# A fused decay attention and MLP kernel: another order for the opening, and SyncE's requests in written order

## The chip, the cores and the metric

The kernel runs on one core of a Trainium2 chip as one launch. The core has five engines with queues of their own: TensorE (PE: matmuls, with weight loads PEld), VectorE (DVE), ScalarE (ACT), GpSimd (POOL) and SyncE (SP), which here does nothing but issue DMA requests. The metric is the device time of a run in microseconds, the median of three runs for the kernel before.

## The reference

Attention over 8 batches of 8 heads, 576 positions and 64 dimensions, then a two-layer MLP over the 4608 tokens.

```python
scores = scale * np.matmul(q, k.transpose(0, 1, 3, 2))
log_f = np.log(np.clip(f, 0.0001, 1.0))
cum = np.cumsum(log_f, axis=-1)
decay = cum[:, :, :, None] - cum[:, :, None, :]
scores = np.where(causal, -1000000000.0, scores + decay)
scores = scores - np.max(scores, axis=-1, keepdims=True)
attn = np.exp(scores)
attn = attn / (np.sum(attn, axis=-1, keepdims=True) + 1e-09)
x = np.matmul(attn, v)          # then heads side by side: 4608 x 512
h = np.maximum(x @ w_in, 0.0)   # w_in 512 x 2048
out = h * h @ w_out             # w_out 2048 x 512
```

## The kernel before

**Data.** There are 64 heads. q and k of a head arrive transposed, side by side (64 x 2 x 576). Heads 0 to 13 ("whole", `NWHOLE = 14`) use two tiles each: `rounded` (name `rk`, q and k rounded to the float32r type by a casting DMA that POOL issues, `load_rounded`, L252) for the row maxima, and `whole` (name `rl`, full float32, requested by SP, `load_whole`, L259) for the scores. Below the 64 rows of q and k lie constant rows and decay rows: the running sum of log f, split in a high and a low row, so that one matmul gives scores with their decay. A further row of `whole` takes the row maxima, so that they too come off in the matmul. From head 14 on ("split" heads) q, k and v are cut into rounded parts by the engines (`prep`, `split_v`), and SP loads the raw tile (`load`, L237).

**Decay (`decay`, L134 to L148).** SP loads f for all 64 heads (L132). DVE clamps it (L138), ACT takes the logarithm (L139) and loads the table of the exponential (L142), DVE forms the running sum (L143), its rounded part (L146) and the rest (L147), in the tile `qkraw`. `load_cum` (L240) brings a head's two rows to `rounded` and `whole`: for head 0 straight from that tile, one request a row (L244), for the others from a copy in DRAM (`cum_dr`, stored by `store_cum`, L152; read at L246).

**Row maxima (`max_units`, L303 to L335).** Six units a head. Each is a matmul (L313) into one of two PSUM banks and a masked reduction on DVE (L319, two instructions in the profile) into a column `tcol`; when a block of queries is done SP writes it as a row into `whole`, or into `rounded` for split heads (L325, `rl<-tcol` or `rk<-tcol`). There are five such requests a head.

**Scores.** A head has six units (`NU = 6`), one a slot. `score` (L337) multiplies (L346, the mask at L348; L352 and L355 in split heads) and takes the exponential on ACT (L362); two slots later `av_part` multiplies with v (L411; L388 to L390 in split heads). `finish` divides by the row sums, by way of DRAM (requests L436, L441, L444), for two heads at a time.

**Weights (`weight_ops`, L164).** A generator that takes the 32 blocks of w_in and w_out through five steps each, on ACT (`wmag`, L181), DVE (L192, L197, L202, L204), then a rounded copy on ACT (L209) and the rest on POOL (L210). Each step ends in a `yield`; the requests (`stage`, L172, 512 KB each) stand in the fourth step and run `DEPTH` blocks ahead.

**MLP.** `mlp1` (L471; matmuls L477) and `mlp2` (L491; L500) run in half steps that `fill` places between the attention's work from slot 60 on; output goes out by SP (L507).

**What sets the order.** The code writes work slot by slot, from slot -12 on: `score`, `av_part`, `finish`, then the events of the slot's first half, weight steps (`cv`), MLP work, and the second half's. In slots -12 to -7 there is one weight step a slot, in -6 to -1 two, in 0 to 47 1.2, after that 2.5 (`RATES`, L549). `MAXIMA` (L555) places the units of row maxima of head h at half slots from `(h - 1) * NU`: those of head 0 in slots -6 to -4, of head 1 in slots 0 to 2. At the end `in_order` (L18) ties each instruction of PE, ACT, DVE and POOL to the one written before it on the same engine. SP is not in that list: a scheduler places its requests.

**The opening, L92 to L158 and L635 to L644.** POOL writes the masks `mz` and `eye`, the constant columns of `vhs`, and the constant rows of `whole[0]`, `rounded[1]` and `whole[1]` (`constant_rows`, L115: two memsets and, for `whole`, a select), and only then issues the casting loads of heads 0 and 1. DVE writes those of `rounded[0]`. SP requests f, the first weights, q and k of head 0 and, after the decay, the decay rows.

Of the kernel before, what the change touches and what calls it, by code (L numbers as in the profile page):

```python
# [9 lines left out]
F32 = mybir.dt.float32  # L10
F32R = mybir.dt.float32r
I32 = mybir.dt.int32
BF16 = mybir.dt.bfloat16
AF = mybir.ActivationFunctionType
ALU = mybir.AluOpType


def in_order(tc, engines):  # L18

    last = {}  # L20
    for i in tc.nc.cur_bb.bb.instructions:
# [12 lines left out]
def decay_attention_relu2_kernel(  # L34
# [18 lines left out]
    nc = tc.nc  # L53

    NH, D, _, S = qk.shape
    P = 2 * D
# [25 lines left out]
    def bank(use):  # L82
# [6 lines left out]

    MW = 448  # L90
    mz = cpool.tile([P, MW], BF16, name="mz")
    nc.gpsimd.memset(mz, 0.0)  # L92
    nc.gpsimd.affine_select(
        out=mz[:, MW - P:], in_=mz[:, MW - P:], pattern=[[-1, P]],
        compare_op=ALU.is_ge, fill=-1e9, base=0, channel_multiplier=1,
    )

    eye = wk.tile([P, 448], F32, name="p").bitcast(BF16)[:, :P]
    nc.gpsimd.memset(eye, 0.0)
    nc.gpsimd.affine_select(  # L100
        out=eye, in_=eye, pattern=[[-1, P]],
        compare_op=ALU.not_equal, fill=1.0, base=0, channel_multiplier=1,
    )

    rounded = [cpool.tile([P, 2, S], F32R, name=f"rk_{i}") for i in range(2)]
    whole = [wk.tile([P, 2, S], F32, name="rl") for _ in range(2)]

    vhs = [cpool.tile([P, NJ, D + 2], F32R, name=f"vh_{i}") for i in range(2)]  # L110

    def f32(x):
        return x if x.dtype == F32 else x.bitcast(F32)

    def constant_rows(engine, x, ones=True):  # L115

        engine.memset(f32(x[D:, 0]), -1.0 / SCALE)
        engine.memset(f32(x[D:, 1]), 0.0)
        if ones:
            k = f32(x[D:, 1])  # L120
            nc.gpsimd.affine_select(
                out=k, in_=k, pattern=[[0, S]], compare_op=ALU.not_equal, fill=1.0, base=-2,
                channel_multiplier=1,
            )


    cum_dr = dr.tile([NH, 2, S], F32, name="cum_dr", bufs=1)
    fr = wk.tile([P, NCC, S], F32, name="xt0", bufs=1)
    cum = []

    def load_f():
        nc.sync.dma_start(out=fr[:NH, 0, :], in_=f)  # L132

    def decay():  # L134
        ft, zt, ct = (fr[:NH, i, :] for i in range(3))
        nc.vector.memset(zt, 0.0)
        constant_rows(nc.vector, rounded[0], False)
        nc.vector.tensor_scalar(ft, ft, 1e-4, 1.0, ALU.max, ALU.min)  # L138
        nc.scalar.activation(out=ft, in_=ft, func=AF.Ln)  # L139
        warm_exp = wk.tile([P, 8], F32, name="tcol")  # L140
        nc.vector.memset(warm_exp[:, :1], 0.0)
        nc.scalar.activation(out=warm_exp[:, :1], in_=warm_exp[:, :1], func=AF.Exp)  # L142
        nc.vector.tensor_tensor_scan(ct, zt, ft, 0.0, ALU.add, ALU.add)  # L143
        chl = wk.tile([P, 2, S], F32R, name="qkraw", bufs=1)
        ch, cl = chl[:, 0, :], chl[:, 1, :]
        nc.vector.tensor_copy(out=ch[:NH], in_=ct)  # L146
        nc.vector.tensor_tensor(out=cl[:NH], in0=ct, in1=ch[:NH].bitcast(F32), op=ALU.subtract)  # L147
        cum.extend(x.bitcast(F32) for x in (ch, cl))  # L148

    def store_cum():  # L150
        for i, x in enumerate(cum):
            nc.sync.dma_start(out=cum_dr[:, i, :], in_=x[:NH])  # L152

    for x in vhs:
        nc.gpsimd.memset(x[:, :, D:D + 2].bitcast(F32), 1.0)
    constant_rows(nc.gpsimd, whole[0])
    constant_rows(nc.gpsimd, rounded[1], False)
    constant_rows(nc.gpsimd, whole[1])  # L158


    NW = 2 * NF
    split_w = []

    def weight_ops():  # L164

        staged, mags = {}, {}

        def stage():
            i = len(staged)
            if i < NW:  # L170
                raw = staged[i] = wk.tile([P, 2 * DM], I32, name=f"w{i}", bufs=1)
                nc.sync.dma_start(out=raw, in_=(w_in, w_out)[i % 2][i // 2].bitcast(I32))  # L172
# [12 lines left out]
        yield  # L185
        magnitude(0)
        yield
        for i in range(NW):
            low, high = words(i)
            mag = mags.pop(i)  # L190

            nc.vector.tensor_scalar(mag, mag, MAG_LOW, MAG_HIGH, ALU.max, ALU.min)  # L192
            yield
            w = wk.tile([P, DM], F32, name="osb")
            wi = w.bitcast(I32)

            nc.vector.tensor_scalar(  # L197
                wi, mag.bitcast(I32), 3, 0x3FFFFFFF, ALU.logical_shift_left, ALU.bitwise_and,
            )
# [4 lines left out]
            nc.vector.scalar_tensor_tensor(wi, low, 29, wi, ALU.logical_shift_right, ALU.bitwise_or)  # L204
            while len(staged) < min(i + 1 + DEPTH, NW):
                stage()
            yield
            hl = wk.tile([P, 2, DM], F32R, name=f"w{i}", bufs=1)
            nc.scalar.copy(out=hl[:, 0], in_=w)  # L209
            nc.gpsimd.tensor_tensor(out=hl[:, 1], in0=w, in1=hl[:, 0].bitcast(F32), op=ALU.subtract)  # L210
            split_w.append(hl)
            yield
# [6 lines left out]
    def convert(n):  # L219

        for _ in range(n):
            next(weights, None)
# [7 lines left out]
    NU = len(UNITS)  # L230
# [8 lines left out]

    def load_cum(h, k):  # L240

        if h == 0:
            for i, c in enumerate(cum):
                nc.sync.dma_start(out=f32(k[D + i:D + i + 1, :]), in_=c[h:h + 1])  # L244
        else:
            nc.sync.dma_start(out=f32(k[D:D + 2, :]), in_=cum_dr[h])  # L246

    def load_rounded(h):

        x = rounded[h % 2]  # L250
        state[h] = dict(r2=x[:, 0], kl0=x[:, 1], p={})
        nc.gpsimd.dma_start(out=x[:D], in_=qk[h])  # L252
# [293 lines left out]

    RATES = (1, 2, 1.2, 2.5)  # L549
    LAG = 2  # L550
    NA = H * NU

# [58 lines left out]
    def at(n, half, do, *args):  # L611
        events.setdefault((n, half), []).append(lambda: do(*args))
# [6 lines left out]
    for h in range(NH):  # L619
        split = h >= NWHOLE  # L620
        if split:
            at((h - 2) * NU + LOAD, 0, load, h)
            for part in range(4):
                at((h - 1) * NU + SPLIT[part], 1, prep, h, part)
        else:
            if h > 1:
                at((h - 3) * NU + 3, 0, load_rounded, h)
                at((h - 2) * NU + 5, 1, load_whole, h)
        at((h - 1) * NU + VLOAD, 1, load_v, h)
        at((h - 1) * NU + VSPLIT, 1, split_v, h)  # L630
        for i, x in enumerate(MAXIMA[split]):
            at((h - 1) * NU + int(x), int(2 * x) % 2, max_unit, h, i)
    for b in range(B):
        at(ready[b] - 2, 0, split_x, b * S // T, b + 1)
    load_f()  # L635
    load_rounded(0)
    convert(1)
    load_whole(0)
    decay()
    load_cum(0, rounded[0][:, 1])  # L640
    load_cum(0, whole[0][:, 1])
    store_cum()
    load_rounded(1)
    load_whole(1)  # L644
    for n in range(-2 * NU, last_slot + 1):
        live = 0 <= n < len(slots)
        split_last()
        if live:
            h, u = slots[n]
# [21 lines left out]
    while halves[0] < 2 * NCHUNK * NF:  # L671
        mlp_half(B)
    mlp2(*steps[-1])
    in_order(tc, [getattr(mybir.EngineType, e) for e in ("PE", "Activation", "DVE", "Pool")])


# [37 lines left out]
```

## Time and profile before

| | us |
|---|---|
| median of 3 runs (lowest to highest) | 1255.66 (1254.82 to 1255.89) |
| the profiled execution | 1255.36 |
| its span, first to last instruction | 1253.3 |
| PE busy | 1193.5 (95%) |
| DVE busy | 785.1 (63%) |
| ACT busy | 702.0 (56%) |
| POOL busy | 372.4 (30%) |

The mean granted TensorE clock of the execution is 0.995. In a profile line of the timeline the first number is the start in microseconds from the span's beginning, the second the length, then the engine (a q after its name marks its request queue), the line of the kernel, the operation, and `out<-in` by tile names without their numbers. In brackets stands how long the engine was idle before, and what ended that. A row of waits reads: who waited for what, total, times, longest.

### The profile page before, as it was taken

The numbers are of one execution on the slowest core, as the hardware profiler recorded it, in microseconds if no ns is written. First come the engines' busy times: TensorE is split into PE (matmuls) and PEld (weight loads), VectorE is DVE, ScalarE is ACT, GpSimd is POOL, SyncE is SP. The second block draws the span as 40 slices with busy tenths as digits, with TensorE's granted clock in tenths as the row PEclk, the third lists the DMA queues.
The fourth block names the chain that finished last, engine by engine and source line by source line (L and its number), as shares of the span: only waits on it lengthen the run. The fifth ranks groups of instructions, "written<-read, shape, count | busy, mean of one in ns | idle before, by whom it ended". The sixth has DMA issues, their size and how long they took to land.

```text
span 1253.3 us, 23182 instructions
## 1 busy us (share of the span) xinstructions
PE 1193.5 (95%) x7652; PEld 1051.8 (84%) x7652; DVE 785.1 (63%) x2042; ACT 702.0 (56%) x1720; POOL 372.4 (30%) x512
## 2 busy tenths in 40 slices
PE   3877899999999999999999999999999999999998
PEld 2544687888989899999899989998998989999997
DVE  7658776666666767666656566667665766532332
ACT  3545455556666666665565556666666666632332
POOL 4323223333333333333322233334333333200000
PEclk9999999999999999999999999999999999999999
DMA  8857631112121112121201121211121212000000
GB/s 199 193 129 176 177 87 26 51 32 57 41 55 33 48 37 57 40 57 26 55 18 52 31 57 32 55 34 52 40 57 41 57 41 52 17 27 1 18 18 17
DMA packets 115639, 71.90 MB, mean 57 GB/s; under 512 B 97384, under 2 KB 97384, under 8 KB 115520
## 3 DMA queue, kind: packets, MB, share of 16 engines
q1 hardware_dynamic: 114400, 66.30, 21.7%
q0 software_dynamic: 1120, 4.13, 1.5%
q8 instruction: 61, 1.00, 0.3%
q14 instruction: 58, 0.48, 0.1%
HBM read 60.20 MB, written 9.88 MB: 56 GB/s over the span
## 4 chain that ended last, share of the span: by engine, by line
PE 63%; ACT 1%; issue 1%; POOL 1%; DMA 0%; DVE 0%; SPq 0%; POOLq 0%; DVEq 0%; ACTq 0%
PE bank L477 25%; PE bank L500 24%; PE bank L388 3%; PE bank L355 2%; PE bank L390 2%; PE bank L389 2%; PE bank L313 2%; PE bank L352 2%; DMA den<-rdr 0%; ACT ph L377 0%; ACT den L426 0%; ACT r L485 0%; ACT p L362 0%; POOL v L299 0%; ACT rl L281 0%
## 5 line engine op out<-in xcount | busy, mean ns | idle before, releaser
L500 PE MATMUL bank<-w,gh 128*128 128x512 f32 x1152 | 413.8, 400 | 0.0
L477 PE MATMUL bank<-xh,w 128*128 128x256 f32 x2304 | 330.7, 286 | 4.9 <-DVE tcol L319 4.9
L378 DVE TENSOR_TENSOR pl<-p,ph 128x320 fp32r<-128x320 f32 (+4 forms) x300 | 186.9, 623 | 206.6 <-ACT ph L377 197.1
L477 PEld LDWEIGHTS bank<-xh,w 128*128 128x128 f32 x2304 | 301.2, 190 | 13.8 <-DVE tcol L319 5.3
L500 PEld LDWEIGHTS bank<-w,gh 128*128 128x128 f32 x1152 | 217.6, 189 | 39.0
L485 ACT ACTIVATE r<-bank 128x256 f32<-128x256 f32 x288 | 110.4, 383 | 211.7 <-PE bank L477 198.3
L500 PE MATMUL bank<-w,gl 128*128 128x512 f32 x576 | 227.1, 394 | 0.2 <-DVE gl L488 0.2
L486 DVE TENSOR_TENSOR g<-r 128x256 f32<-128x256 f32 x288 | 127.3, 442 | 144.2 <-ACT r L485 143.4
L364 POOL TENSOR_SCALAR_AFFINE_SELECT p<-p 128x128 f32<-128x128 f32 (+1 forms) x250 | 81.5, 326 | 454.2 <-ACT p L362 313.5
L377 ACT CAST ph<-p 128x320 fp32r<-128x320 f32 (+4 forms) x300 | 124.4, 415 | 148.9 <-POOL p L364 147.1
L477 PE MATMUL bank<-xl,w 128*128 128x256 f32 x1152 | 185.3, 283 | 0.0
L319 DVE CUSTOM_DVE_ANT_0 bank<-bank,mz 128x256 f32<-128x256 f32 (+4 forms) x320 | 133.7, 432 | 45.9 <-PE bank L313 44.5
L477 PEld LDWEIGHTS bank<-xl,w 128*128 128x128 f32 x1152 | 158.9, 191 | 0.0
L362 ACT ACTIVATE p<-bank 128x320 f32<-128x320 f32 (+4 forms) x300 | 115.8, 386 | 71.7 <-PE bank L355 67.3
L488 DVE TENSOR_TENSOR gl<-g,gh 128x256 fp32r<-128x256 f32 x288 | 128.9, 448 | 35.7 <-ACT p L362 0.9
L313 PE MATMUL bank<-rk 66*128 66x320 f32 (+9 forms) x384 | 111.8, 318 | 24.8 <-DMA rk<-qkraw 13.4
L487 ACT ACTIVATE gh<-r 128x256 fp32r<-128x256 f32 x288 | 120.5, 418 | 9.1
L500 PEld LDWEIGHTS bank<-w,gl 128*128 128x128 f32 x576 | 109.3, 190 | 14.3 <-DVE gl L488 0.9
L313 PEld LDWEIGHTS bank<-rk 66*128 66x128 f32 (+3 forms) x384 | 68.7, 185 | 40.1 <-DVE tcol L319 17.1
L388 PE MATMUL bank<-pl,vh 128*65 128x320 f32 (+4 forms) x350 | 99.4, 284 | 1.6 <-ACT den L426 1.4
L389 PE MATMUL bank<-ph,v 128*64 128x320 f32 (+4 forms) x350 | 94.8, 271 | 0.0
L390 PE MATMUL bank<-ph,vh 128*65 128x320 f32 (+4 forms) x350 | 93.0, 271 | 0.0
(71 smaller groups left out, 1498.2 us busy)
## 6 DMA issues: line engine op xcount, KB each, us to landing
qkraw<-in_qk SPq DMA_DIRECT2D x50, 288.0 KB
v<-in_v SPq DMA_DIRECT2D x64, 160.0 KB
den<-rdr SPq DMA_DIRECT2D x64, 144.0 KB
out<-osb SPq DMA_DIRECT2D x36, 256.0 KB
w<-in_w_in SPq DMA_DIRECT2D x16, 512.0 KB
w<-in_w_out SPq DMA_DIRECT2D x16, 512.0 KB
rl<-in_qk SPq DMA_DIRECT2D x14, 288.0 KB
rk<-in_qk POOLq DMA_DIRECT2D x14, 288.0 KB, 4.7
```

What stands on the lines that cost most here:

```text
L313: nc.tensor.matmul(ps[:m, :n], st["r2"][:rows, q0:q0 + m], st["kl0"][:rows, k0:k0 + n], start=True, stop=True,)
L319: nc.vector.tensor_tensor_reduce(out=ps[:m, :n], in0=ps[:m, :n], in1=mz[:m, mo:mo + n], op0=ALU.add, op1=ALU.min, scale=-1.0, scalar=init, ...
L377: nc.scalar.copy(out=ph[:kn, :n], in_=p[:kn, :n])
L378: nc.vector.tensor_tensor(out=pl[:kn, :n], in0=p[:kn, :n], in1=ph[:kn, :n].bitcast(F32), op=ALU.subtract,)
L388: nc.tensor.matmul(acc[:D + 1, o], vh, pl[:kn, i], start=first, stop=False)
L389: nc.tensor.matmul(acc[:D, o], vl, ph[:kn, i], start=False, stop=False)
L390: nc.tensor.matmul(acc[:D + 1, o], vh, ph[:kn, i], start=False, stop=last)
L477: nc.tensor.matmul(ph[:, :T], w[:, s, cc], x[:, cc, :], start=(cc == 0 and k == 0), stop=(cc == NCC - 1 and k == 2),)
L486: nc.vector.tensor_tensor(out=g, in0=r, in1=r, op=ALU.mult)
L487: nc.scalar.activation(out=gh, in_=r, func=AF.Square)
L488: nc.vector.tensor_tensor(out=gl, in0=g, in1=gh.bitcast(F32), op=ALU.subtract)
L500: nc.tensor.matmul(po, g[:, ts], w[:, s], start=(fc == 0 and k == 0), stop=(fc == NF - 1 and k == 2),)
```

## The change

The opening is written in another order.

- POOL issues the casting loads of heads 0 and 1 first. The masks follow (`masks()`), then, held by an added dependency until the decay's last DVE instruction, the constant rows of `rounded[1]`, those of `whole[1]`, and the constant columns of `vhs`.
- DVE writes the constant rows of `whole[0]` as well as of `rounded[0]`, ahead of the clamp of f; the select on `whole[0]` stays on POOL.
- A head's two decay rows go in one request, from the tile in SBUF for heads 0 and 1, and the store of all rows to DRAM is one request, behind those of head 1.
- The first two weights are requested where they were. Then blocks run two, three and four ahead instead of four at once, so that requests move behind the row maxima of head 0.
- The row maxima of head 1 move three slots ahead, to slots -3 to -1.
- Weight steps a slot: 1.5 instead of 2 in slots -6 to -1, 1.3 instead of 1.2 in slots 0 to 47.
- `in_order` takes SP in: its requests are issued in the written order throughout.

```diff
-    nc.gpsimd.memset(mz, 0.0)
-    nc.gpsimd.affine_select(out=mz[:, MW - P:], ...)
     eye = wk.tile([P, 448], F32, name="p").bitcast(BF16)[:, :P]
-    nc.gpsimd.memset(eye, 0.0)
-    nc.gpsimd.affine_select(out=eye, ...)
+    def masks():
+        nc.gpsimd.memset(mz, 0.0)
+        nc.gpsimd.affine_select(out=mz[:, MW - P:], ...)
+        nc.gpsimd.memset(eye, 0.0)
+        nc.gpsimd.affine_select(out=eye, ...)
...
+    ft, zt, ct = (fr[:NH, i, :] for i in range(3))
...
     def decay():
-        ft, zt, ct = (fr[:NH, i, :] for i in range(3))
-        nc.vector.memset(zt, 0.0)
-        constant_rows(nc.vector, rounded[0], False)
         nc.vector.tensor_scalar(ft, ft, 1e-4, 1.0, ALU.max, ALU.min)
...
-        cum.extend(x.bitcast(F32) for x in (ch, cl))
+        cum.append(chl.bitcast(F32))
+        return tc.nc.cur_bb.bb.instructions[-1]

     def store_cum():
-        for i, x in enumerate(cum):
-            nc.sync.dma_start(out=cum_dr[:, i, :], in_=x[:NH])
-
-    for x in vhs:
-        nc.gpsimd.memset(x[:, :, D:D + 2].bitcast(F32), 1.0)
-    constant_rows(nc.gpsimd, whole[0])
-    constant_rows(nc.gpsimd, rounded[1], False)
-    constant_rows(nc.gpsimd, whole[1])
+        nc.sync.dma_start(out=cum_dr, in_=cum[0][:NH])
...
-            while len(staged) < min(i + 1 + DEPTH, NW):
+            while len(staged) < min(i + 1 + min(2 + i, DEPTH), NW):
...
-        if h == 0:
-            for i, c in enumerate(cum):
-                nc.sync.dma_start(out=f32(k[D + i:D + i + 1, :]), in_=c[h:h + 1])
+        if h < 2:
+            nc.sync.dma_start(out=f32(k[D:D + 2, :]), in_=cum[0][h:h + 1])
...
-    RATES = (1, 2, 1.2, 2.5)
+    RATES = (1, 1.5, 1.3, 2.5)
...
         for i, x in enumerate(MAXIMA[split]):
-            at((h - 1) * NU + int(x), int(2 * x) % 2, max_unit, h, i)
+            if h == 1:
+                x -= 3
+            at((h - 1) * NU + math.floor(x), int(2 * x) % 2, max_unit, h, i)
...
     load_f()
     load_rounded(0)
+    load_rounded(1)
     convert(1)
     load_whole(0)
-    decay()
+    nc.vector.memset(zt, 0.0)
+    constant_rows(nc.vector, whole[0])
+    constant_rows(nc.vector, rounded[0], False)
+    masks()
+    scanned = decay()
     load_cum(0, rounded[0][:, 1])
     load_cum(0, whole[0][:, 1])
+    begin = len(tc.nc.cur_bb.bb.instructions)
+    constant_rows(nc.gpsimd, rounded[1], False)
+    tc.add_manual_dep(tc.nc.cur_bb.bb.instructions[begin], scanned.name, ...)
+    load_cum(1, rounded[1][:, 1])
+    constant_rows(nc.gpsimd, whole[1])
+    load_whole(1)
     store_cum()
-    load_rounded(1)
-    load_whole(1)
+    for x in vhs:
+        nc.gpsimd.memset(x[:, :, D:D + 2].bitcast(F32), 1.0)
...
-    in_order(tc, [getattr(mybir.EngineType, e) for e in ("PE", "Activation", "DVE", "Pool")])
+    in_order(tc, [getattr(mybir.EngineType, e) for e in ("PE", "Activation", "DVE", "Pool", "SP")])
```

More of the change, by code (lines that the diff above doesn't have):

```diff
@@ L91, in decay_attention_relu2_kernel @@
     mz = cpool.tile([P, MW], BF16, name="mz")
[L92 to L96, printed above, removed]
-    eye = wk.tile([P, 448], F32, name="p").bitcast(BF16)[:, :P]
-    nc.gpsimd.memset(eye, 0.0)
[L100 to L103, printed above, removed]
+    eye = wk.tile([P, 448], F32, name="p").bitcast(BF16)[:, :P]
+    def masks():
+        nc.gpsimd.memset(mz, 0.0)
+        nc.gpsimd.affine_select(
+            out=mz[:, MW - P:], in_=mz[:, MW - P:], pattern=[[-1, P]],
+            compare_op=ALU.is_ge, fill=-1e9, base=0, channel_multiplier=1,
+        )
+        nc.gpsimd.memset(eye, 0.0)
+        nc.gpsimd.affine_select(
+            out=eye, in_=eye, pattern=[[-1, P]],
+            compare_op=ALU.not_equal, fill=1.0, base=0, channel_multiplier=1,
+        )
     rounded = [cpool.tile([P, 2, S], F32R, name=f"rk_{i}") for i in range(2)]
@@ L129, in decay_attention_relu2_kernel @@
     cum = []
+    ft, zt, ct = (fr[:NH, i, :] for i in range(3))
     def load_f():
-        nc.sync.dma_start(out=fr[:NH, 0, :], in_=f)
+        nc.sync.dma_start(out=ft, in_=f)
     def decay():
-        ft, zt, ct = (fr[:NH, i, :] for i in range(3))
-        nc.vector.memset(zt, 0.0)
-        constant_rows(nc.vector, rounded[0], False)
         nc.vector.tensor_scalar(ft, ft, 1e-4, 1.0, ALU.max, ALU.min)
@@ L636, in decay_attention_relu2_kernel @@
     load_rounded(0)
+    load_rounded(1)
     convert(1)
     load_whole(0)
-    decay()
+    nc.vector.memset(zt, 0.0)
[3 more added lines that the diff above has]
+    scanned = decay()
     load_cum(0, rounded[0][:, 1])
     load_cum(0, whole[0][:, 1])
+    begin = len(tc.nc.cur_bb.bb.instructions)
+    constant_rows(nc.gpsimd, rounded[1], False)
+    tc.add_manual_dep(
+        tc.nc.cur_bb.bb.instructions[begin], scanned.name,
+        mybir.DependencyInfo(mybir.DependencyClass.Sync, mybir.DependencyReason.DATA),
+        reason="the decay first",
+    )
+    load_cum(1, rounded[1][:, 1])
+    constant_rows(nc.gpsimd, whole[1])
+    load_whole(1)
     store_cum()
-    load_rounded(1)
-    load_whole(1)
+    for x in vhs:
+        nc.gpsimd.memset(x[:, :, D:D + 2].bitcast(F32), 1.0)
     for n in range(-2 * NU, last_slot + 1):
```

## The prediction

> **What bounds the kernel now.** I read the page's head, then busy time by stage, to see where TensorE idles.
>
> ```profile
> span 1253.3 us, 23182 instructions
> ...
> 0.00:13.40 13.40, 0.00 (x0) 0.00 (x0) 9.36 (x12) 5.29 (x7) 7.67 (x21) 1.00 0.80 206
> ...
> 13.40:23.00 9.60, 3.04 (x7) 1.58 (x7) 8.18 (x22) 2.96 (x5) 3.17 (x5) 1.00 0.84 220
> 23.00:31.55 8.55, 8.55 (x31) 5.97 (x31) 6.15 (x17) 3.31 (x8) 2.90 (x4) 1.00 0.81 167
> 31.55:40.60 9.05, 8.47 (x42) 6.03 (x41) 5.76 (x19) 5.71 (x15) 2.57 (x4) 1.00 0.96 196
> 40.60:50.10 9.50, 6.76 (x35) 4.67 (x33) 6.58 (x20) 5.65 (x13) 2.73 (x4) 1.00 0.61 148
> ...
> 300.00:600.00 300.00, 299.32 (x2012) 270.86 (x2011) 202.72 (x549) 187.77 (x468) 105.34 (x148) 1.00 0.19 45
> 600.00:1000.00 400.00, 398.80 (x2675) 360.45 (x2675) 262.63 (x705) 247.78 (x614) 135.33 (x189) 1.00 0.18 44
> ```
>
> After each stage's length come PE, weight loads, DVE, ACT and POOL, then the granted clock, the DMA share and GB/s. From 300 to 1000 us PE is busy for 698 of 700 us. There nothing but an earlier start helps: a microsecond that PE's fixed queue gains ahead of it is a microsecond at the end. The idle time lies at the front: all of the first 13.4 us, and 6.6 of the next 9.6. The waits of PE say for what (total, times, longest):
>
> ```profile
> PE bank L313 <- DMA rk<-qkraw: 13.4, 1, 13.4
> PE bank L346 <- DMA rl<-tcol: 10.8, 4, 4.7
> PE bank L313 <- DVE tcol L319: 9.8, 15, 1.6
> PE bank L346 <- DMA w<-in_w_out: 5.3, 1, 5.3
> PE bank L477 <- DVE tcol L319: 4.9, 1, 4.9
> ```
>
> The first row is the opening: PE's first matmul (row maxima of head 0) waits for the decay rows. The fourth is the first score, which waits for the row maxima's transfers (the transfer named there is queued among them). The second and fifth lie between 50 and 135 us: later heads waiting for their row maxima, and the first MLP step. The change addresses the first and the fourth. The opening in order of time (start, length, engine):
>
> ```profile
> 0.82 0.47 POOL L92 MEMSET mz<- 128x448 bf16 x1 [0.29 <-POOLq L704]
> 0.82 0.57 SPq L132 DMA_DIRECT2D xt<-in_f  x1
> 1.00 0.54 DVE L136 MEMSET xt<- 64x576 f32 x1 [1.00 <-PEq L704]
> ...
> 1.70 0.54 DVE L117 MEMSET rk<- 64x576 f32 x1 [0.16 <-issue]
> 1.87 0.29 POOL L100 TENSOR_SCALAR_AFFINE_SELECT p<-p 128x128 bf16<-128x128 bf16 x1
> ...
> 2.31 0.54 DVE L118 MEMSET rk<- 64x576 f32 x1
> ...
> 3.47 0.66 POOL L121 TENSOR_SCALAR_AFFINE_SELECT rl<-rl 64x576 f32<-64x576 f32 x1
> 3.48 3.04 DVE L138 TENSOR_SCALAR xt<-xt 64x576 f32<-64x576 f32 x1 [0.64 <-DMA xt<-in_f]
> 4.08 0.58 POOL L117 MEMSET rk<- 64x576 f32 x1
> ...
> 6.28 0.76 POOL L121 TENSOR_SCALAR_AFFINE_SELECT rl<-rl 64x576 f32<-64x576 f32 x1
> ...
> 6.99 1.21 POOL L252 DMA_DIRECT2D rk<-in_qk  x2
> ...
> 9.13 1.30 SPq L244 DMA_DIRECT2D rk<-qkraw  x2
> 9.14 0.75 DVE L147 TENSOR_TENSOR qkraw<-xt,qkraw 64x576 fp32r<-64x576 f32 x1
> 9.81 0.41 DVE L192 TENSOR_SCALAR wmag<-wmag 128x512 f32<-128x512 f32 x1
> ...
> 11.45 0.69 DVE L204 SCALAR_TENSOR_TENSOR osb<-w,osb 128x512 int32<-128x512 int32 x1
> ...
> 13.43 0.82 PE L313 MATMUL bank<-rk 128*128 128x256 f32 x2 [13.43 <-DMA rk<-qkraw]
> ...
> 14.13 0.43 DVE L319 CUSTOM_DVE_ANT_0 bank<-bank,mz 128x256 f32<-128x256 f32 x1 [1.99 <-PE bank L313]
> ...
> 16.39 0.43 SPq L172 DMA_DIRECT2D w<-in_w_in  x1
> ...
> 16.92 1.81 SPq L325 DMA_DIRECT2D rl<-tcol  x3
> ...
> 18.25 0.13 DVE L319 DVE_READ_ACCUMULATOR2_ANT tcol<- 64x1 f32 x1
> ...
> 18.66 1.29 POOL L210 TENSOR_TENSOR w<-osb,w 128x512 fp32r<-128x512 f32 x1 [4.39 <-ACT w L209]
> 18.76 1.51 DVE L197 TENSOR_SCALAR osb<-wmag 128x512 int32<-128x512 int32 x1
> ...
> 23.00 1.41 PE L346 MATMUL bank<-rl 128*128 128x320 f32 x2 [5.30 <-DMA w<-in_w_out]
> ```
>
> What to see: q and k of head 0 are requested at 6.99, behind POOL's constants. The clamp of f (L138) takes 3.04 us where a larger operation of its kind (L192) takes 0.41: it ends at 6.52, when POOL's train of four memsets (4.08 to about 6.2) is over. The three row maxima for the first score are requested from 16.92, behind a weight at 16.39, and serve PE only at 23.00.
>
> **The change part by part.** I carry one path to slot 6, the first score of head 1. The profiled execution took 1255.36 us (2.06 around its span), 0.30 under the median 1255.66, so differences go onto the median.
>
> *Decay.* DVE now does five memsets ahead of the clamp: 1.00, then 0.70 and 0.61 apart, so done near 4.1; f has landed at 3.48. POOL first issues the two requests (1.21, from 0.82 to 2.0), then the select on whole[0] once DVE's third memset is over (2.85 + 0.66 = 3.5), then the masks (0.82 to 2.16 in the rows, 1.3): 4.8. If the clamp waits for POOL again it runs from 4.8 to 5.2, against 6.52: 1.3 us gained. What follows it to the end of L147 is unchanged (6.52 to 9.89), so the decay ends at 8.55. Two small requests fewer for head 0 save SP some 0.6 each, beside other work.
>
> *First matmul.* Before, 3.5 us pass from the second decay request (9.9) to PE (13.43). Request to use took 2.66 for f (0.82 to 3.48). From 8.6 that gives 11.3 to 12.1, so DVE could begin row maxima (0.70 after PE) at 12.0 to 12.8. Head 0's q and k, asked for 6 us earlier, are no limit any more.
>
> *DVE behind the decay.* Four steps on weight 0 come first (9.81 to 12.14: 2.33). POOL's constants for rounded[1] and whole[1], four memsets and a select, are now started by the decay's end: just beside those steps, two of which are of the clamp's kind. Nothing here shows this meeting; the nearest row is L138, held for 2.6 us. Bounds: 0 (DVE first) and 2.9 (the train from 4.08 to 7.04). I take the four memsets, 2.1. The first maximum is then at 8.55 + 2.33 + 2.1 = 13.0, up to 13.8 with the select; I take 13.4. The cover that the waiting PE gave these four steps before is thus gone: DVE becomes the limit here.
>
> [...]
>
> *Row maxima of head 0.* Before 14.13 to 18.38, 4.25. The rate of 1.5 instead of 2 steps a slot takes one 0.6 us step out: 3.6. POOL's subtraction for weight 0 can now meet a weight step; such a meeting cost 1.1 (L197 took 1.51 beside it, and L192, of the same size, 0.41). I take half: 4.1, so done at 17.5. Requests: the third weight is now asked for after the decay's requests, ahead of the maxima, and the next two behind them. The third maximum is found near 16; with 2.7 to 3.5 us it is there by 19.5.
>
> *Row maxima of head 1,* moved three slots ahead, come before the first score on PE and DVE: one weight step (0.6), 3.6 for the maxima, 1.0 for a meeting: until 22.7 on DVE. PE's last matmul of them is over some 1.1 earlier, by estimate, as a maximum (0.43) and a step (0.6) follow it on DVE. First score at 21.6, against 23.00. The earlier transfers alone would have allowed 19.5; the rest of that gain is spent on this moved work.
>
> *Slots 0 to 5.* This stage was filled by PE, and the same stage restricted to L313 shows what leaves it:
>
> ```profile
> 23.00:31.55 8.55, 2.68 (x6) 1.61 (x6) 1.00 0.81 167
> ```
>
> 8.55 − 2.68 = 5.87. If ACT's part shows between scores it may be 1 longer. Slot 6 comes at 21.6 + 5.9 = 27.5 against 31.55: **4.1 us gained.** Ends: no meeting with POOL at all and the first maximum at 12.4 gives 12.4 + 3.6 + 0.6 + 3.6 − 1.1 = 19.1 (beside 19 for the transfers), 6.5 gained; all meetings in full give 13.8 + 4.7 + 0.6 + 3.6 + 2.2 − 1.1 = 23.8, 1.9 gained, and 0.9 with the 1 us.
>
> *Rates behind.* Up to slot 48 the weight steps sum to 1 + 6 + 12 + 57.6 = 76.6 before and 1 + 6 + 9 + 62.4 = 78.4 now: some 0.1 step more per slot and none on PE. I count it at nothing; its cover is DVE's idle time (5.76 busy of 9.05 us). Without it: 4.8 steps at 0.58 (2.33 / 4) over 48 slots, 2.8 lost, of which 3 steps are saved ahead. The vh constants move behind the decay and are used from head 14 on.
>
> *SP in trace order.* Read against the loops, the requests up to about 143 us are already in that order, but for one weight and the decay's store in the opening. Later PE has next to no idle time that SP could end (1.9 us in the 700 above). Last request of a row maximum and the score that needs it, of one split head, and SP's longest wait:
>
> ```profile
> 622.30 0.55 SPq L325 DMA_DIRECT2D rk<-tcol  x1
> ...
> 626.68 0.31 PE L352 MATMUL bank<-rk 67*128 67x320 f32 x1
> ...
> SPq L436 <- ACT ph L377: 250.0, 43, 7.2
> ```
>
> The room is 4.4 us, of which a transfer needs some 2.7. I count zero: the written order puts the denominator requests (L436) a slot ahead of the maxima and the broadcast (L444) behind them. Ends: nothing gained, since PE waits for none of it; a loss in the third rival.
>
> Sum: 1255.66 − 4.1, and a little for the busy DMA engines: **1251.7**.
>
> **The rivals.** *POOL does not hold DVE* (chance 0.18). For it: DVE reaches its weight steps without a wait, POOL by a semaphore. Against it: L138. 1255.66 − 6.5 = 1249.2. [...]
>
> *The start is earlier and is given back* (0.23). For it: from 31.55 to 40.60 the DMA engines are 0.96 busy, and the same bytes are asked for 4 us sooner; later heads already wait for row maxima, 10.8 in four waits, 2.7 each. One such wait more at head 2 or 3 leaves 4.1 − 2.7 = 1.4: 1254.3. Against it: the DMA share falls to 0.61 in the next head, and one weight less has been asked for at slot 6.
>
> *SP's written order delays the maxima of split heads* (0.07), the slower side. Place: the wait of L352 for rk<-tcol, from 143 us on. If a request ahead (L436, whose wait reaches 7.2) holds the last maximum by more than the room of 4.4 − 2.7 = 1.7, PE stalls in each of 50 heads. From 0.13 us a head beyond that room (6.6 / 50) the kernel is slower by 2.5; at 0.2 it is 1255.66 − 4.1 + 10 = 1261.6. Against it: slots are 3.7 us long there and the order favours the maxima.
>
> **How the numbers follow.** The forecast, 1251.7 with its own range 1250.0 to 1253.1, has 0.52. A measurement of this kernel tells about 0.2%, 2.5 us, from no change. Faster: 0.52 + 0.18 = 0.70; same: the second rival, 0.23; slower: 0.07. The range reaches from below the first rival, 1248.2, to over the second, 1255.2, which takes in the bounds 6.5 and 0.9.
>
> **What would show it.** q and k requested by 2 us; the clamp over near 5.2; first matmul by 12.1, first score near 21.6, head 1's first score near 27.5, with the maxima of head 1 ahead of the first score; L192 or L197 near 9 us with 2 to 3 us; later waits as before. Wrong: the clamp still held past 6 us; the first score at 23; new waits of L346 for rl<-tcol at heads 2 and 3; any wait of L352 for rk<-tcol.

## The result, and the profile after

The changed kernel took 1263.87 us (median of 4 runs, 1261.1 to 1265.3) against 1255.24 (1254.28 to 1255.89) for the kernel before (4 runs): a ratio of 1.0066, with an interval of 1.0042 to 1.009. It is 8.6 us slower where a gain of 4 us, 1251.7, had been forecast, and outside the range. The profiled execution of the changed kernel took 1262.6 us (span 1260.9), 1.3 under its median.

The stages of the span, cut at the first score of heads 0, 1, 4, 10, 17, 18 and 63. Columns: start and end, length, then busy time and count of PE, weight loads, DVE, ACT and POOL, then the granted clock, the DMA share and GB/s. The changed kernel:

```profile
core 0 of [0], span 1260.9 us
...
13.40:22.23 8.83, 5.82 (x13) 3.04 (x13) 7.79 (x26) 1.28 (x2) 3.16 (x4) 1.00 0.69 153
22.23:30.50 8.27, 8.27 (x27) 4.98 (x27) 5.29 (x12) 3.85 (x10) 1.79 (x3) 1.00 0.85 244
30.50:61.90 31.40, 23.08 (x114) 16.05 (x112) 21.32 (x57) 17.40 (x42) 11.19 (x14) 0.95 0.83 191
61.90:131.10 69.20, 53.18 (x223) 36.66 (x223) 44.13 (x123) 35.56 (x81) 20.47 (x24) 0.87 0.68 158
131.10:275.02 143.92, 134.78 (x815) 114.73 (x815) 93.46 (x237) 77.05 (x184) 44.61 (x50) 0.98 0.28 72
275.02:297.44 22.42, 18.57 (x112) 16.19 (x111) 13.45 (x31) 10.54 (x27) 7.25 (x9) 0.92 0.16 41
297.44:1089.28 791.84, 786.99 (x5285) 712.02 (x5283) 513.82 (x1417) 494.98 (x1229) 270.61 (x382) 1.00 0.19 44
```

The same heads in the kernel before:

```profile
31.55:60.17 28.62, 22.90 (x113) 16.04 (x112) 18.23 (x56) 16.72 (x41) 9.22 (x12) 1.00 0.83 184
60.17:127.81 67.64, 50.84 (x223) 33.96 (x223) 45.48 (x122) 35.22 (x81) 20.96 (x26) 0.95 0.66 158
127.81:272.55 144.74, 135.00 (x816) 114.81 (x815) 99.83 (x237) 75.65 (x185) 46.18 (x51) 0.99 0.30 78
272.55:292.62 20.07, 18.50 (x113) 16.15 (x111) 14.51 (x32) 10.53 (x27) 6.37 (x9) 0.91 0.16 42
292.62:1081.86 789.24, 786.85 (x5285) 711.66 (x5283) 526.04 (x1416) 494.69 (x1229) 272.34 (x383) 1.00 0.19 44
```

Head 1 begins 1.1 us earlier (30.50 against 31.59; the table cuts at 31.55, as the prediction does). Heads 1 to 10 lose 4.3 (31.40 + 69.20 against 28.62 + 67.64), heads 10 to 17 win 0.8, head 17 alone loses 2.35, heads 18 to 63 another 2.6. That the last of these stages lost at all, with PE 0.99 busy in it, is the surprise: it is the stretch in which "nothing but an earlier start helps". PE's idle time in it went from 2.4 to 4.9. The waits of PE in the changed kernel (total, times, longest):

```profile
PE bank L338 <- DMA rl<-tcol: 15.5, 5, 5.8
PE bank L305 <- DMA rk<-qkraw: 13.4, 1, 13.4
PE bank L305 <- DVE tcol L311: 7.6, 13, 2.2
PE bank L338 <- issue: 5.6, 3, 2.4
PE bank L305 <- DVE rk L272: 5.4, 5, 1.6
```

Lines have moved by eight here: L338 is the score of whole heads, L305 the matmul of the row maxima. The first row lies at heads 4 to 10, and grew from 10.8. The last was 0.3 in one wait before (`rk L280`): split heads waiting for DVE's rounded q and k. Nothing waits for `rk<-tcol`.

The opening of the changed kernel:

```profile
1.33 1.21 POOL L244 DMA_DIRECT2D rk<-in_qk  x2 [0.80 <-POOLq L715]
...
4.09 0.45 DVE L137 TENSOR_SCALAR xt<-xt 64x576 f32<-64x576 f32 x1
...
7.16 0.75 DVE L146 TENSOR_TENSOR qkraw<-xt,qkraw 64x576 fp32r<-64x576 f32 x1
7.94 0.72 SPq L236 DMA_DIRECT2D rk<-qkraw  x1
...
9.16 0.76 DVE L185 TENSOR_SCALAR wmag<-wmag 128x512 f32<-128x512 f32 x1 [1.25 <-ACT wmag L174]
...
10.76 1.03 DVE L195 SCALAR_TENSOR_TENSOR osb<-w,osb 128x512 int32<-128x512 int32 x1
...
13.42 0.82 PE L305 MATMUL bank<-rk 128*128 128x256 f32 x2 [13.42 <-DMA rk<-qkraw]
14.12 0.43 DVE L311 CUSTOM_DVE_ANT_0 bank<-bank,mz 128x256 f32<-128x256 f32 x1 [1.61 <-PE bank L305]
...
22.23 2.48 PE L338 MATMUL bank<-rl 128*128 128x320 f32 x4
...
28.47 0.92 PE L338 MATMUL bank<-rl 128*128 128x448 f32 x2
```

q and k are asked for at 1.33, the clamp is over at 4.54, the decay at 7.91, and still PE starts at 13.42, as before (13.43): the decay rows, asked for at 7.94, are used 5.5 us later.

### The profile page after: what moved, and what is told of

Same layout as the page of the kernel before. It is cut to its first block, busy times and chain, and to the rows that moved or that the text cites. A ratio compares the mean times of both kernels' runs of the same rounds, so it can differ in the third digit from the quotient of the medians.

```text
span 1260.9 us, 23142 instructions
## 1 busy us (share of the span) xinstructions
PE 1198.5 (95%) x7652; PEld 1055.3 (84%) x7652; DVE 765.8 (61%) x2044; ACT 703.6 (56%) x1720; POOL 370.3 (29%) x510
## 3 DMA queue, kind: packets, MB, share of 16 engines
HBM read 60.19 MB, written 9.88 MB: 56 GB/s over the span
## 4 chain that ended last, share of the span: by engine, by line
PE 80%; DVE 6%; issue 4%; DMA 4%; ACT 3%; POOL 2%; SPq 1%; DVEq 0%; POOLq 0%; ACTq 0%
PE bank L469 31%; PE bank L492 28%; PE bank L380 4%; PE bank L305 3%; PE bank L382 3%; PE bank L347 3%; PE bank L381 3%; PE bank L344 2%; PE bank L338 2%; PE bank L403 2%; DMA den<-rdr 1%; DVE bank L311 1%; DMA rl<-tcol 1%; DVE g L478 1%; DMA qkraw<-in_qk 1%
## 5 line engine op out<-in xcount | busy, mean ns | idle before, releaser
L370 DVE TENSOR_TENSOR pl<-p,ph 128x320 fp32r<-128x320 f32 (+4 forms) x300 | 181.3, 604 | 212.1 <-ACT ph L369 204.5
L478 DVE TENSOR_TENSOR g<-r 128x256 f32<-128x256 f32 x288 | 134.5, 467 | 149.6 <-ACT r L477 148.5
L305 PE MATMUL bank<-rk 66*128 66x320 f32 (+9 forms) x384 | 113.7, 324 | 28.4 <-DMA rk<-qkraw 13.4
L305 PEld LDWEIGHTS bank<-rk 66*128 66x128 f32 (+3 forms) x384 | 69.5, 187 | 44.5 <-DVE tcol L311 13.6
```

The costliest lines, as they stand in the source:

```text
L305: nc.tensor.matmul(ps[:m, :n], st["r2"][:rows, q0:q0 + m], st["kl0"][:rows, k0:k0 + n], start=True, stop=True,)
L370: nc.vector.tensor_tensor(out=pl[:kn, :n], in0=p[:kn, :n], in1=ph[:kn, :n].bitcast(F32), op=ALU.subtract,)
L478: nc.vector.tensor_tensor(out=g, in0=r, in1=r, op=ALU.mult)
```

## The experiments

The medians of the kernel before were 1254.35, 1255.38, 1254.78 and 1256.25 in the four sets of runs (25, 22, 31 and 31 runs); each ratio is the one on record against the set's own runs, which is not the quotient of the two medians and can differ from it by 0.1%. Stage times are of the profiled executions, one for each kernel, at the first score of a head, against the kernel before (its first scores of heads 10, 17, 18 and 63: 127.81, 272.55, 292.62, 1081.86). The theories by letter, where an expectation uses one: A, the weight rates cost the time; C, the written order delays the broadcast of the denominators; F, PE's first matmul waits in a queue of large transfers; H, weights delay the row maxima of heads 4 to 10; J, the denominators of whole heads do; K, a gained start is lost in later waits for row maxima.

### Rates or SP's order

**e1**, the change with the old rates.

```diff
-    RATES = (1, 1.5, 1.3, 2.5)
+    RATES = (1, 2, 1.2, 2.5)
```

> The changed kernel with the weight rates of before (2 and 1.2 steps a slot instead of 1.5 and 1.3). Theory A (the rate of 1.3 moves the weight requests between the row maxima of heads 3 and 8, PE then waits longer and its granted clock drops): the waits of PE for row maxima at heads 4, 6 and 9 fall from 4.8, 5.8 and 3.1 us to 2.4, 4.7 and 0.5, head 10 starts no later than in the kernel before (127.8), the time is 1256 to 1258. Theory B (SyncE's written order is the cause): 1262 to 1264, as the changed kernel.

1261.31, ratio 1.0062 (1.0042 to 1.0082). At head 17 it stands 0.35 ahead, at head 18 2.9 behind, at head 63 5.25 behind. So the rates are not the main cause.

**e2**, the change without the written order of SP:

```diff
-    in_order(..., ("PE", "Activation", "DVE", "Pool", "SP")])
+    in_order(..., ("PE", "Activation", "DVE", "Pool")])
```

> The changed kernel with SyncE's requests left to the scheduler. Theory A: head 10 still starts near 131, and only what is lost behind head 16 (5 us: waits of PE for the DVE copies of q and k) returns: 1258 to 1260. Theory B: the whole loss is gone, 1253 to 1256. If SyncE's order costs nothing: 1262 to 1264.

1254.62, ratio 0.9999 (0.9982 to 1.0017). The first matmul comes only at 15.61, but the loss at head 18 is gone (3.4 ahead of before).

**e3**, the kernel before with the new rates; **e4**, the kernel before with SP in written order.

```diff
-    RATES = (1, 2, 1.2, 2.5)
+    RATES = (1, 1.5, 1.3, 2.5)                                  # e3
...
-    in_order(..., ("PE", "Activation", "DVE", "Pool")])
+    in_order(..., ("PE", "Activation", "DVE", "Pool", "SP")])   # e4
```

> The kernel before with the new rates alone. Theory A: waits of 4 us and more at two or three heads and a granted clock near 0.990, time 1258 to 1262. Theory B: 1255, unchanged.

1253.51, ratio 0.9986 (0.9966 to 1.0006): no effect that can be measured.

> The kernel before with SyncE in written order alone. Theory A: nothing changes up to 143 us, where the requests already stand in that order; behind it PE waits about 1 us each at heads 18, 50 and 58 for the copies of q and k, whose load is asked for later: 1257 to 1260. Theory B: 1262 to 1264. If the order costs nothing: 1255.

1266.06, ratio 1.0087 (1.0061 to 1.0113). SP's order alone, on the old opening, costs 11.7 us (4 runs). A part lies in the opening, where the first score comes 3.15 us later, behind a wait that is put down to a head's decay rows from DRAM (`cum_dr`). PE's row in the timeline of e4:

```profile
26.15 1.40 PE L346 MATMUL bank<-rl 128*128 128x320 f32 x2 [8.78 <-DMA rk<-cum_dr]
```

Another 4.5 us are lost up to head 10, and 5.8 behind head 17's first score: head 17 takes 22.45 here, 22.42 in the changed kernel and 18.38 in e2.

### What at head 18?

The timeline of SP and POOL before head 18 (start, length), kernel before:

```profile
265.14 0.35 SPq L441 DMA_DIRECT2D rdr<-cmp  x1
...
267.62 1.19 SPq L444 DMA_DIRECT2D den<-rdr  x2
268.90 0.55 SPq L325 DMA_DIRECT2D rk<-tcol  x1
...
271.71 1.44 POOL L447 TENSOR_TENSOR xt<-xt,den 128x576 f32<-128x576 f32 x1 [1.20 <-DMA den<-rdr]
```

And SP, POOL, DVE and PE in the changed kernel (L433, L436 and L439 are the old L441, L444 and L447):

```profile
267.65 0.35 SPq L433 DMA_DIRECT2D rdr<-cmp  x1
268.10 3.53 SPq L317 DMA_DIRECT2D rk<-tcol  x3
271.72 0.55 SPq L230 DMA_DIRECT2D qkraw<-in_qk  x1
272.36 1.19 SPq L436 DMA_DIRECT2D den<-rdr  x2
...
277.44 1.43 POOL L439 TENSOR_TENSOR xt<-xt,den 128x576 f32<-128x576 f32 x1 [4.47 <-DMA den<-rdr]
...
278.91 0.56 DVE L456 CAST xh<-xt 128x768 fp32r<-128x768 f32 x1 [3.67 <-POOL xt L439]
...
281.25 0.38 PE L305 MATMUL bank<-rk 66*128 66x256 f32 x1 [1.62 <-DVE rk L272]
...
284.59 0.63 PE L305 MATMUL bank<-rk 66*128 66x320 f32 x1 [2.23 <-DVE tcol L311]
```

The broadcast of the denominators (`den<-rdr`) was issued 2.48 us behind the store it reads (`rdr<-cmp`), and now 4.71: it is written behind the third row maximum, for which SP waits, and behind the q and k of a later head (64 x 2 x 576 values, 288 KB). It also lands later: from its issue's end to POOL's division 2.9 us pass before, 3.9 now. POOL waits 4.47 for it, DVE's cast of x, next in DVE's fixed order, 3.67 for POOL, and PE for DVE in two waits, where the kernel before has one of 1.6. The waits of DVE for POOL's division between 262 and 1090 us, in the changed kernel and in the kernel before (L464 and L447 there):

```profile
DVE xh L456 <- POOL xt L439: 15.0, 6, 3.7
...
DVE xh L464 <- POOL xt L447: 6.8, 4, 2.0
```

The six stand at heads 17, 25, 33, 41, 49 and 57, one a batch of eight heads; so the loss shows there. Two ways to free one request from SP's chain, the others staying in order:

```diff
+    free = set()            # names left out of the chain
...
                 nc.sync.dma_start(out=den[...], in_=st["rdr"][i:i + 1].broadcast_to([D, S]))
+                let()           # e5: den<-rdr;  e6: the load of qkraw instead
```

> The changed kernel with the old rates and with SyncE in written order but for the broadcasts of the denominators (den from rdr), which the scheduler may place. Theory C (behind 143 us the written order holds these broadcasts behind a row maximum that is not ready and behind the load of q and k; DVE's cast of x and then PE wait): the 3.3 us lost between heads 17 and 18 and the 1.1 us at head 50 are gone, 1255 to 1257 against 1261.3. Theory D (the later load of q and k for the next head is what PE waits for): no change, 1260 to 1262.

**e5** (with the old rates): 1255.94, ratio 1.001 (0.9989 to 1.0031). Head 17 takes 18.28: its loss is gone. (The profiled execution, 1263.73, was the slowest of its ten, so its earlier stages tell nothing.)

> The same with the loads of q and k of the split heads left to the scheduler instead, the broadcasts in written order. Theory C: no change, 1260 to 1262, head 18 still 3 us behind the kernel before. Theory D: 1255 to 1257.

**e6** (with the old rates): 1258.84, ratio 1.0025 (1.0009 to 1.004). The loss at head 17 stays (from 3.9 behind to 6.9), but from there to head 63 it shrinks by 1.3, where e1 loses 2.3 more. DVE's waits for POOL at heads 25, 33, 49 and 57 are 1.3 to 1.5 here and 2.2 to 2.6 in e1. So the q and k loads are a smaller part of the loss, later on, and the time lies between the two theories.

**e9**, e1 with the broadcast written one slot earlier, SP wholly in written order:

```diff
-    DIVIDE = (2, 5, 8, 11), (2, 4, 6, 7)
+    DIVIDE = (2, 5, 8, 11), (2, 4, 5, 7)
```

> The changed kernel with the old rates, SyncE wholly in written order, and the broadcast of the denominators of split heads written one slot earlier (slot 4 of a head instead of 5), ahead of the last row maximum. Theory C (the written place of the broadcast is the loss, not the fixed order as such): no loss between heads 17 and 18, 1255 to 1257 against 1261.3. Rival (a fixed order costs wherever it stands, since SyncE waits at its head): 1260 to 1262.

1254.29, ratio 0.9987 (0.9968 to 1.0006): one number in a table takes back 7.0 us. **e13** makes the same edit in the change as it was, and **e16** in e4 (the kernel before with SP in written order).

> The changed kernel whole, its own rates kept, with the broadcast of the denominators of split heads written one slot earlier. Theory C carried to the changed kernel: 1254 to 1257 against 1263.9, no loss between heads 17 and 18. If the new rates put their own loss on top (heads 4 to 10 were 4.6 us behind): 1258 to 1260.

1254.40, ratio 0.9986 (0.997 to 1.0002), 9.5 below the median of the changed kernel. SP's requests and POOL's division in its timeline:

```profile
266.60 0.35 SPq L433 DMA_DIRECT2D rdr<-cmp  x1
267.05 1.65 SPq L317 DMA_DIRECT2D rk<-tcol  x2
268.75 1.23 SPq L436 DMA_DIRECT2D den<-rdr  x2
270.10 0.52 SPq L317 DMA_DIRECT2D rk<-tcol  x1
...
272.44 1.67 POOL L439 TENSOR_TENSOR xt<-xt,den 128x576 f32<-128x576 f32 x1 [0.51 <-DMA den<-rdr]
```

And head 17 as a stage of e13, in the columns of the first table of stages:

```profile
273.97:292.26 18.29, 16.96 (x113) 14.88 (x111) 13.55 (x32) 10.57 (x27) 5.78 (x9) 1.00 0.17 46
```

The broadcast follows the store by 2.15 and POOL waits 0.51. Head 17 takes 18.29 instead of 22.42, and at head 63 the kernel is 0.3 behind before instead of 7.4. DVE waits for POOL before none of those casts. A part of head 17's loss is PE's pace: the granted clock of the stage is 0.92 in the changed kernel, 0.91 in the kernel before and 1.00 here, and PE is busy for 18.57, 18.50 and 16.96 us with about the same matmuls. So head 17 of the kernel before, at 20.07, had lost something too.

> The kernel before with SyncE wholly in written order and the broadcast one slot earlier. Theory C: of the 11.7 us that the written order cost there, 5 to 7 return, and the opening's share (first score 3 us later, its store and loads written ahead of the row maxima) stays: 1258 to 1261. If all returns: 1254 to 1256.

1258.23, ratio 1.0021 (1.0 to 1.0041): of e4's 11.7 us all but 2 return; the late first score (26.02) stays.

From head 17's first score to head 63's, e13 is 6.1 us shorter than the changed kernel, e9 7.5 shorter than e1, and e16 8.0 shorter than e4. That is what the place of the broadcast is worth. What is left of each difference lies almost wholly in earlier heads, of which both kernels of a pair write at least the first 14 alike, and it goes either way: at head 10 e4 is 7.6 behind the kernel before and e16 2.9, but e1 is 0.5 ahead and e9 2.3 behind.

### The opening, and why it is worth nothing

**e7**, e1 with less ahead of head 0's decay rows: the casting load of head 1, the full-float32 q and k of head 0 and the second weight go behind them.

```diff
-        stage()
+        late.append(stage)      # the second weight
...
     load_rounded(0)
-    load_rounded(1)
     convert(1)
-    load_whole(0)
...
     load_cum(0, rounded[0][:, 1])
-    load_cum(0, whole[0][:, 1])
+    load_whole(0)               # q, k and the decay rows
+    late[0]()
...
-    load_cum(1, rounded[1][:, 1])
+    load_rounded(1)             # q, k and the decay rows
```

> The changed kernel with the old rates; ahead of the decay only f, q and k of head 0 for the row maxima and one weight are requested; the second weight, the whole tile of head 0 and q and k of head 1 follow the decay rows of head 0. Theory F (the decay rows wait in SyncE's DMA queue behind 1.3 MB that shares the engines with the casting loads): the first matmul comes at 10.3 to 11.5 instead of 13.4, the first maximum on DVE near 12.5, head 1's first score 1.5 to 2.5 us earlier than 30.5. Rival G (a small transfer of the opening takes 3.5 to 5.5 us whatever is queued): first matmul at 13.4 as before.

1265.87, ratio 1.0088. The first matmul comes at 9.88 instead of 13.42 in the changed kernel, so what was requested ahead of the decay rows was the limit; but DVE then waits for the late second weight, and PE for DVE. PE in the timeline of e7 (its lines are one higher):

```profile
17.61 0.64 PE L306 MATMUL bank<-rk 128*128 128x320 f32 x1 [5.27 <-DVE tcol L312]
```

**e11** keeps SP's order only up to slot 0; **e12** is e11 with head 1's casting load and `whole[0]` behind the decay rows.

```diff
+        if n == 0:                       # e11, e12
+            written = len(tc.nc.cur_bb.bb.instructions)
...                                       # SP's requests behind that place
+    free = {i.name for i in ...instructions[written:] if i.engine == ...SP}
-    in_order(tc, [..., "SP")])
+    in_order(tc, [..., "SP")], free)     # are left out of the chain
...
-    load_rounded(1)                      # e12 (and e14)
-    load_whole(0)
     load_cum(0, rounded[0][:, 1])
-    load_cum(0, whole[0][:, 1])
+    load_whole(0)                        # q, k and the decay rows
...
-    load_cum(1, rounded[1][:, 1])
+    load_rounded(1)                      # q, k and the decay rows
```

> The changed kernel with SyncE in written order up to slot 0 alone, behind that left to the scheduler. If the written order costs only behind 143 us: opening as in the changed kernel (first score 22.2, head 1 at 30.5), no loss at head 18, 1252 to 1256. If it costs in slots 0 to 60 too, the same with less at head 10 than the 3.3 us of the changed kernel: 1249 to 1252.

> As the run before it, but with the casting load of head 1 and the whole tile of head 0 requested behind the decay rows of head 0, both first weights ahead of them. Theory F: the first matmul comes near 10.0 instead of 13.4; since DVE no longer waits for the second weight, the first maximum comes near 12.7, head 1's first score 1 to 2 us before 30.5, and the time is 1 to 2 us under the run before it. Rival (the row maxima of head 1 and DVE set slot 0 whatever PE's start is): head 1's first score stays within 0.5 us of 30.5.

1253.93 (0.9986, 0.9968 to 1.0004) and 1254.16 (0.9992, 0.9974 to 1.0009). First matmuls at 15.62 and 14.53: requests left free are pulled ahead into the opening (in e11 two more weights, at 3.06 and 3.72), so neither has the opening that it was to have. No loss at head 18 in either.

**e14** is the cleanest opening: e13 with the loads moved as in e12, the second weight where it was. In the texts of e14 and e15 the other run that is meant is e13.

> As the run before it, with the casting load of head 1 and the whole tile of head 0 requested behind the decay rows of head 0, SyncE wholly in written order. Theory F: first matmul near 10.0 to 11, head 1's first score 1 to 3 us before that of the run before it; if that start is worth its time at the end, 1252 to 1254; if later waits of PE take it back (theory K: from head 3 on each head waits for transfers that do not start earlier), within 1 us of the run before it.

1254.85, ratio 0.9991 (0.9977 to 1.0005). PE in its timeline, at the first matmul and the first scores of heads 1 and 4:

```profile
9.89 0.82 PE L305 MATMUL bank<-rk 128*128 128x256 f32 x2 [9.89 <-DMA rk<-qkraw]
...
28.45 0.81 PE L338 MATMUL bank<-rl 128*128 128x320 f32 x2
...
60.04 1.41 PE L338 MATMUL bank<-rl 128*128 128x320 f32 x2 [5.07 <-DMA rl<-tcol]
```

Three quarters of the forecast gain exist here: head 1 starts 3.1 us before the old kernel's, head 3 3.35. At head 4 PE waits 5.07 for row maxima, where the kernel before waited 2.37, and starts only 0.1 ahead; at head 10 it is 0.3 behind.

**e15** is e13 without the three slots by which head 1's maxima were moved.

```diff
-            if h == 1:
-                x -= 3
```

> As the first of these runs, with the row maxima of head 1 back in slots 0 to 2. By the forecast's sum moving them ahead was worth 2.7 us of PE in slots 0 to 5 less 1 to 2 of a later first score: head 1's first score 1 to 2 us later, the time 0 to 2 us more. Theory K: same time within 1 us.

1254.00, ratio 0.9986 (0.9973 to 0.9999). The first score comes at 19.08 instead of 22.41, head 1's at 32.19 instead of 32.24: in these two executions the move changes where PE waits, not when head 1 begins. One execution says little of that, since the same opening began head 1 at 30.50 in the changed kernel and at 32.24 in e13; the whole times, 1254.00 and 1254.40, say the same. The interval of e15 ends just below the old kernel's time, and none of the others (e9, e11 to e14) is set apart from that time.

### The waits of heads 4 to 10

**e8**, the change with weights requested in slots 0 to 77 only once a head's last row maximum has been (slots with `n % NU` of 2, 3, 4).

```diff
-            while len(staged) < min(i + 1 + min(2 + i, DEPTH), NW):
-                stage()
+            want[0] = min(i + 1 + min(2 + i, DEPTH), NW)
+            if hold[0]:
+                catch_up()               # stages up to want[0]
...
+        hold[0] = n < 0 or n >= (NWHOLE - 1) * NU
...
+        if n >= 0 and n % NU in (2, 3, 4):
+            catch_up()
```

> The changed kernel, its rates kept, with weight requests held in slots 0 to 77 until the last row maximum of a head has been requested. Theory H (a weight of 512 KB ahead of a row maximum in SyncE's queue is what PE waits for at heads 4, 6 and 9): the waits of 4.8, 5.8 and 3.1 us fall under 2.5 each, the granted clock rises from 0.988 to 0.993, 1255 to 1259 with the loss behind head 17 still there. Rival I (the waits come from DVE's pace and the denominators' transfers): they stay, 1262 to 1265.

1264.19, ratio 1.0075 (1.0049 to 1.0101). The waits stay (5.76 at head 4). SP in its timeline, ahead of that wait (L327 the row maxima, L446 the broadcast):

```profile
50.87 0.51 SPq L327 DMA_DIRECT2D rl<-tcol  x1
56.47 1.13 SPq L446 DMA_DIRECT2D den<-rdr  x2
57.69 1.83 SPq L327 DMA_DIRECT2D rl<-tcol  x3
```

SP stands still for 5 us ahead of a broadcast, with three row maxima behind it.

**e10**, the kernel before with the denominators of whole heads later.

```diff
-    DIVIDE = (2, 5, 8, 11), (2, 4, 6, 7)
+    DIVIDE = (4, 6, 9, 11), (2, 4, 6, 7)
```

> The kernel before with the denominators of whole heads handled in slots 3, 5, 2 and 4 of a head instead of 1, 4, 1 and 4, so that their requests stand behind the first three row maxima. Theory J (SyncE waits in front of the row maxima for these requests' data, and PE for the row maxima): the waits at heads 3, 4, 6 and 8 (2.2, 2.4, 4.7, 2.6 us) fall under 1 each and the time to 1246 to 1250. Rival (DVE's pace or the DMA engines' load sets those waits): they stay, 1254 to 1256.

1257.72, ratio 1.0019 (1.0004 to 1.0034). Of J the waits come true and the time does not. PE no longer waits before the first score of any of heads 3 to 8. The two waits of scores for row maxima that are left, 5.6 in all, stand at heads 0 and 2. But PE's waits for DVE (L313) grow from 9.8 to 18.1, and the first MLP step's from 4.9 to 6.7. H is not borne out.

## Why the prediction was wrong, by its own steps

**SP in trace order: counted at zero, and it decided.** It named the fact ("the broadcast (L444) behind them") and then priced only the row maxima, whose room of 4.4 us was indeed enough: no `L344 <- rk<-tcol` wait appears. The broadcast had no room, and the old trace said so: POOL already waited 1.20 us for it at 271.71, with DVE's cast of x behind POOL. The third rival (0.07) had the sign, and with 1261.6 nearly the size, but that nearness is luck, for its place was wrong: not 0.2 us in each of 50 heads, but 2.35 at head 17 (4.1 against the 18.3 of an undisturbed one), and 2.6 in all over heads 18 to 63. e13 shows the cause, and e9 and e16 show it twice more: written order kept, one broadcast moved, the loss of heads 17 to 63 gone. The reading that up to 143 us the requests are in that order "but for one weight and the decay's store" also put a cost at nothing: on the old opening the written order made the first score 3.15 (e4) and 3.0 us (e16) later.

**Decay.** Forecast to end at 8.55, ended at 7.91: the clamp was not held by POOL at all (0.45, beside a memset and a select; 3.04 before).

**First matmul.** 2.7 to 3.5 us from request to use were taken from f, which is requested first, and from the old second decay row, requested at 9.9; it was 5.5, behind two weights and the q and k of `whole[0]` on SP's queue and beside POOL's two casting loads. With the loads of `rounded[1]` and `whole[0]` moved behind, 7.94 to 9.89 (e14). "Head 0's q and k are no limit any more" was right; what came ahead with them was the limit: from request to use 5.5 us with both loads ahead, 1.95 without. By what way these loads hold the decay rows is not shown.

**DVE behind the decay.** 2.1 us of meetings with POOL were taken; the four steps took 3.35 for 2.33 (9.16 to 12.51), 1.0 more, and hid behind the wait for the rows. They also began at 9.16, behind ACT's step on the weight, and not with the decay's end. The first rival, "POOL does not hold DVE", was half right, and worth nothing, since the decay rows set the time.

**First score and slots 0 to 5.** First score forecast 21.6, came at 22.23. Then 8.27 us for six slots, not 5.87: the sum took PE's busy share of L313 off the stage's length, as if the rest closed up. It does not. By line, PE's busy times in the old stage add up to 12.01 us (L313 2.68, L346 5.35, L411 2.70, L348 1.28) in 8.55, so the lines overlap, and the share of one can't be taken off. And PE runs slowly there. In the changed kernel each of the score matmuls of 128x320 from 22.9 to 24.0 takes 0.74 us, and from 30.9 on 0.43. The stage's row prints a granted clock of 1.00, but the trace holds no record of the clock before 28.33. In e13 the slow pace lasts longer: its pair of 128x448 at 28.77 takes 1.70, where that of the changed kernel at 28.47 takes 0.92, and its six slots take 9.83. They take 6.92 at the least, in e2. Gain at head 1: 1.1 in this execution, not 4.1; e15 shows no worth of the moved maxima.

**The start is given back.** Even the 3.1 us of e14 are lost by head 4 in its profiled execution. The second rival (0.23) described this nearly: a longer wait for row maxima, 2.7 more (5.07 for 2.37), at head 4 and not at head 2 or 3. Alone it would have meant no measurable change. e13 and e14 show that: the whole change without the late broadcast is worth nothing that the runs can tell from zero.

**Rates.** Counted at nothing; e1 and e3 agree.

Not settled: what sets the pace of heads 4 to 10. e8 left the waits for row maxima, and e10, on the kernel before, took them away without a gain. The pace also varies between executions of kernels that write these heads alike, as e1 and e9 do (0.5 ahead and 2.3 behind at head 10).

## What to carry to other kernels

When an engine's requests are put into written order, go through every request and ask who waits for it and with what room, not only for those on the bound engine's own path: a request that some engine already waits for has no room. An engine off the bound (POOL, 30% busy) can hold up the bound one where a fixed order on a third engine, here DVE's, stands between them: POOL waited 4.47 us, DVE 3.67 for POOL, and PE 1.62 and 2.23 for DVE. And a faster start is worth what the next fixed wait leaves of it, in e14 0.1 us of 3.1: before working on an opening, look at the waits behind it (here those of heads 4 to 10). And a line's busy time can't be taken off a stage's length until the busy times of all lines have been added up and compared with that length.

## What was not expected of the hardware

One wait of PE was paid for twice. In the changed kernel PE stops before 61.90 and then finds the clock at half. Two stretches of it, in the columns of the stages above, the wait and what follows:

```profile
57.06:61.90 4.84, 0.01 (x1) 0.04 (x1) 0.54 (x1) 1.14 (x3) 3.07 (x3) 0.71 1.14 256
61.90:66.00 4.10, 4.10 (x10) 2.73 (x11) 1.24 (x5) 1.27 (x3) 0.00 (x0) 0.52 0.44 121
```

The granted clock was 0.52 for the first 4.1 us of work behind a wait of 4.84. In steps of 0.5 us it reads 1.00 up to 59.0, 0.50 from 59.5 to 65.5 and 1.00 from 66.0. Over heads 4 to 10 the mean clock was 0.87, against 0.95 in the kernel before, and PE's busy time for the same 223 matmuls 53.18 against 50.84: that is 2.3 of the 4.3 us lost over heads 1 to 10.

The length of the wait alone did not decide. A wait of 2.37 in the kernel before, until 60.17, was followed by a clock of 1.00 (60.17 to 63.00), and one of 2.38 in the changed kernel, until 106.35, by 0.52 (107.00 to 110.40). So two waits of one length cost differently here; what decided between these two, and what brings the clock back, is not shown.
